# Multiples of the identity built on chip, first loads on two queues, three added groups of small matmuls and a new written-out order, in a fused attention and state-space kernel

## The chip, the cores and the metric

The kernel runs on one core of a Trainium2 chip. A core has five engines, each with an instruction stream of its own that it works through in order: PE (TensorE, matmuls), DVE (VectorE, elementwise work), ACT (ScalarE, activation functions and copies), POOL (GpSimd; here memsets and the issue of software DMAs) and SP (SyncE, issue of DMAs). They share an on-chip memory, SBUF, of 128 partitions and a small accumulator memory, PSUM, of eight banks. Streams wait for one another by semaphores. The metric is the device time of one execution in microseconds (us), as the median of several runs; smaller is better.

## The reference, cut to what matters

Two independent branches, whose outputs stand side by side in the last dimension:

```python
def _A_ref(x, wqkv, w_phi, wo):                 # linear attention, 16 heads of 28
    qkv = (x @ wqkv).reshape(B, S, 3, H, Dh)    # S = 2048, D = 448
    pq = einsum("bhsd,hdf->bhsf", q, w_phi)     # the same for k
    phi = concat([softmax(p), softmax(-p)])
    kv = einsum("bhsf,bhsd->bhfd", phi_k, v);  z = phi_k.sum(s)
    o = (phi_q @ kv) / (phi_q @ z + 1e-6)
    return o @ wo
def _B_ref(u, A, Bc, Cc, log_dt, Dskip):        # state-space convolution, 256 states
    K[d, l] = Re sum_n Cc * exp(dt * A * l) * dt * Bc      # l = 0..2047
    y = irfft(rfft(u padded) * rfft(K padded))[:L]         # along the sequence
    return y + u * Dskip
return concat([a, b], axis=-1)
```

All inputs and the output are bf16.

## The kernel before, in words

The convolution is done as a real discrete Fourier transform of 512 points on tiles of 128 partitions. Its parts are named by a label given with `step(...)`:

- **states**: six raw arrays (`rawAre`, `rawAim`, `rawCre`, `rawCim`, `rawBre`, `rawBim`, 448 x 256 each, 224 KB) are transposed and scaled by matmuls against a diagonal matrix `DT` (function `to_states`, label `st...`). `stAre` is what the step sizes act on, `stCre` and `stCim` are copied out of PSUM, `stB0` and `stB1` each read both `rawBim` and `rawBre`. Four products of them on DVE (`cb`) give the starting values. `hlA`, `lowA` (and `hlT`, `lowT`) store the decay in two bf16 parts.
- **phases** (`exps`, `rot`): for eight chunks of 56 channels the decay and the phase of a state are multiplied by 1 to 16. This is a matmul against `PID`, 16 multiples of the identity matrix, held as a 128 x 16 x 128 bf16 tile of 512 KB. Before the change `PID` is loaded from a constant in DRAM (unit 18, line 470), and `ident`, its first slice, by a transfer of its own (line 450).
- **hi, damp, far, build**: tables of powers (complex products on DVE, some of whose adds are accumulating DMAs that POOL issues, `add_to`, line 387), from which `build` makes the convolution kernel on PE.
- **sc / last, ks, conv, inv**: scatter to row positions by small DMAs, the kernel's spectrum, the product with the signal's spectrum (`us`, from `ua`, `ub` and the table `G1`, stored to DRAM and loaded again, `su`), and the inverse transform. The channels go through these in three groups (`GROUPS`, of four, two and two chunks).

The attention branch transposes x in 16 blocks (`xT`, from four loads `xs`, label `inx`), folds `w_phi` into the projections (`fold1` for keys, `fold0` for queries: transposes of `Wqk`, copies, then products with `BD`, a block matrix that four small DMAs, label `bd`, fill from `w_phi`), and then runs keys (`ke`, `kz`, `key`), `keyend` and queries (`qe`, `qz`, `q`). An exponential on ACT stands behind each `ke` and `qe`.

Nothing of the order of work follows from loops. The body builds a list of 1359 units, each with the engines that it may run on; `ORDER` (line 97) is a written-out string of unit numbers with a letter for the engine (P, D, A, G for POOL, S for SP), and `Plan.run` (line 213) emits the units in that order. Addresses in SBUF come from `HOMES`, PSUM banks from `BANKS`; both were written out by the same planner. Tiles share addresses where their lives don't overlap, so a transfer can have to wait until an older tile at its address has been read. The second number in each `plan.add` is the planner's cost, which the chip never sees. In the profile, line 360 is any ordinary matmul, 330 any `tensor_tensor`, 340 any activation, 346 and 351 copies, 384 any plain DMA, 398 and 396 the two forms of `add_to` (by POOL's accumulating DMA, by DVE), 608 the `xT` transposes, 618 the `fold` transposes, 649 the two gathers `ub`.

At the start of the kernel before, SP issues all first loads, in this order: `ldt`, `ident`, `Cim`, `bd`, `Are`, `Bim`, `Cre`, `Bre`, `bd`, x0, `Wqk` (784 KB), `bd`, `PID`, x1, `bd`, `HM`, ua1, ua0, `Aim`, `G1` (1 MB), `Wv`. POOL issues two gathers of 896 KB each in the meantime. `G1` shares an address with `f1`, a tile of the `cb` products. PE's order at the start is: `dt`, `stCim`, `stAre`, `stCre`, `stB0`, `lowA`, `stB1`, four `xT`, the `fold1` and `fold0` transposes, `exps0.1`, the `fold1` products, and so on to the first `ke0`.

Of the kernel before, what the change touches and what calls it, by code (L numbers as in the profile page):

```python
# [11 lines left out]
ACT = mybir.ActivationFunctionType  # L12
# [24 lines left out]
N_TB = 21  # L37
TB_STEP = 2368
# [15 lines left out]
def _dft_tables():  # L54
# [29 lines left out]
    pid = np.eye(128)[:, None, :] * np.arange(1, 17)[None, :, None]  # L84
# [13 lines left out]
0S 15G 24P 1S 5S 16G 19S 2S 7S 23D 25A 26D 54P 55A 4S 27P 29A 6S 52P 33D 53A 32A 30A 56P 34P 165G 57P 58D 20S 61D 8S  # L98
96P 31A 98P 12S 35A 92P 59D 94P 130P 97A 131D 95D 60D 21S 128P 142P 18S 99A 140P 124P 93A 141A 129D 143D 683P 126P
127D 144P 145D 146P 125A 684A 9S 22S 132P 685A 147D 133D 686A 138P 106P 134P 136P 107D 680P 135A 150P 137D 139D 102P  # L100
100P 63D 687A 62D 263P 681A 104P 105D 101D 151D 210G 211G 156S 682A 103D 209S 265A 213D 264A 257P 164S 254P 259A 258A
255A 260P 256A 309P 166G 262A 168D 300P 261A 152P 212D 167D 154P 311A 306P 303P 310A 153D 155D 285G 301A 279P 3S 13S
302A 148P 149D 307A 308A 28P 304A 287P 295P 280D 288D 305A 312P 39A 40A 266P 296D 313D 37A 36A 219P 267D 49A 41D 184P
185A 221P 186P 220A 191P 187A 38D 189P 190D 192A 14S 64D 65D 67G 284P 292P 46A 69D 251P 68D 43A 42A 271P 47A 222A 71G
48D 66D 223S 249P 50P 252A 294A 286A 272A 196P 246P 51A 174P 250A 179P 194P 80A 193S 195A 180A 247A 44D 176P 177A 244P
169P 201P 70D 197A 72D 82A 269G 73D 181P 268P 289D 188S 83D 182A 76D 75G 84D 77D 175D 45A 229P 171P 79D 202A 74D 183S
270A 78D 230A 276P 253S 199P 273D 81A 699D 245A 224P 248S 315G 200A 170A 86A 688P 277G 700D 278A 206P 203S 178S 225A
746D 226P 745D 172A 198S 274P 275P 239P 204P 281D 283P 747D 85A 87A 240A 89D 173S 205A 701G 227A 282P 690A 689A 691P
236P 744S 694A 693A 698S 207A 88D 291P 695A 293G 692A 749D 330P 322P 332A 290P 703D 234P 323G 237A 324A 702D 208S 748D
# [12 lines left out]
381D 862P 1020D 1052P 1021D 1012A 861A 1007A 863D 884S 1061D 1009A 1057A 1058A 415G 1031D 1049P 1078D 1055A 363P 364D
1053A 120P 121D 1032D 367P 1056A 1030D 1051A 1033D 398P 893S 422P 1022G 1054A 892G 890S 1023D 1050A 392P 1024D 900G
406P 1029G 400A 1059S 1062G 1064D 395P 399A 397A 366P 396A 1075G 424A 373D 401P 403A 1063D 402A 371P 430P 1035D 379P
393A 394A 1077D 432A 387P 404P 425P 1025G 372A 426D 380A 405D 1026D 409P 1065G 899G 375P 383P 423G 374P 408A 886S 382P
410A 433P 417P 1178P 1034D 878S 419D 388A 447P 434A 407G 411D 391P 1036G 427D 1180A 390P 1027D 418A 1227P 1067D 435D
1066D 1028G 1179A 412P 1076D 873G 413P 420P 421P 429P 1228A 1231A 1230A 444P 448A 875G 428P 1068G 453P 437P 1229A
1079D 450P 449A 895G 1197D 894S 436P 931S 455A 902G 1181P 454A 445A 452A 1198D 879G 1081D 881S 1080D 1069D 1070D 441D
1071D 1182A 451A 446A 442D 1073D 1037P 1072D 880S 1196G 937S 1184A 1224P 1039P 1185A 882G 1225A 1183A 885S 1226A 439D
1074D 1199G 1082G 1038A 1040A 1189P 1200D 1235P 1201D 950S 1191A 1186P 1188A 1083P 1187A 1195A 17G 1202D 870G 887G  # L130
868G 869S 484P 440D 1203D 1204D 438D 1194A 1205G 1239A 1212G 1190A 866S 1192A 1085P 1215D 485A 1084A 1232P 1193A 864G
1086A 1113S 1088G 1237A 1213D 1233A 874S 1214D 1117S 901G 1238A 943S 1234A 896G 867S 1216D 1207D 1206D 621P 502P 1240A
624P 1217D 508P 1109G 1208D 1218D 1087S 1241A 877S 1210D 1114G 925S 618P 1236A 504A 1209D 563P 503A 1219D 883S 898G
1098S 627P 628A 629A 505P 1211D 619A 1244D 506A 919S 1242G 1243D 626A 1245G 1110S 511P 949S 1222P 163S 623A 904S 625A
1258G 443D 510A 888S 1220P 1259D 162S 509A 513A 1260D 1124G 622A 507A 464P 1261D 920S 897S 512A 876G 620A 560P 903S
1262D 926S 1247D 482P 472P 938S 1221A 1223A 914S 514P 494P 630P 483D 465A 565A 908S 871G 891G 865G 1091S 666P 889S
561A 1246D 564A 515D 158S 516D 495D 631D 473A 667A 872D 1094G 474P 475A 632D 517D 532P 533A 566P 569P 550P 562A 568A
570A 567A 1248G 542P 571A 913S 1264D 456P 457D 1263D 492P 1099S 493A 927P 656P 551A 458D 462P 543A 1097G 928D 907S
1104G 939P 1250D 633D 157S 1120S 646P 522P 1249D 1251D 1252D 1253D 940A 657A 518D 572P 932S 1126S 463A 1090G 944S 160S
600P 636P 637A 578P 579A 1127G 1265G 1112S 601A 1121S 519D 1111S 647A 915P 1093G 929P 530P 930A 523A 951P 921P 1089S  # L140
459D 916A 1119G 580P 581A 540P 933P 1101G 658P 1100S 952A 668P 1254D 1115G 1256D 1255D 541A 659D 520P 945P 922A 531A
460D 1102G 934A 1257D 909P 669A 638P 648P 521A 649A 906G 573D 552P 1266P 574D 534D 1092S 910A 1268P 610P 1107A 634D
1122S 635D 650D 461D 905S 941P 1103S 670D 553A 1108A 1118A 159S 676S 496D 575D 639D 576D 544D 946A 1267A 1269A 1296G
476D 554D 1300A 953P 1095D 486D 524D 911P 935P 611A 912A 660D 1271G 608P 923P 924D 609A 577D 917P 671P 161S 954A 555P
1096S 466D 582D 918A 672A 651P 1293G 1305S 487P 612D 677S 640D 942A 556A 661P 467P 947P 557P 1308S 497P 678S 1116G
936A 1106G 955D 1105S 662A 956D 477P 948A 1276G 468A 1288G 588P 488A 598P 590P 652A 589A 525P 478A 1270G 958G 489P
498A 673P 1303G 490A 1294A 613P 674A 479P 599A 591D 1287S 675A 535P 583P 957D 536A 1275G 1125G 641P 469P 480A 537P
1291G 653P 642A 1286G 526A 558A 1272S 584A 585P 1307S 499P 614A 973D 1299A 1279G 527P 975D 959D 615P 1123S 1283A 654A
960D 491A 1289S 1134P 962D 1138P 1304A 481A 586A 592D 1281S 1273G 528A 961D 1290S 963P 964A 470D 593P 545P 1298G 977G
1285G 974D 976D 538A 1135A 1292S 1295A 1130P 594A 1274S 643P 1128S 500D 1139A 965P 1131D 1306S 1142P 1302A 546A 547P  # L150
1277G 978D 980D 1278D 616A 1280S 966A 1143A 1136P 970P 1282G 679S 595P 979D 1129S 602D 982D 1132P 644A 1137A 1309S
1284G 1144P 1146D 981D 1297A 971A 471A 1140P 1145A 1334D 984D 1311P 1315P 596A 1319P 1141A 1147D 1323P 1316D 1171D
1310S 1148D 1133A 1162D 1163D 990P 1352D 501A 1301S 603P 1317P 1161D 1312A 1320A 983G 1321P 1313P 1150D 968P 1314A
1324A 597S 1149G 991A 1325P 1160D 1327D 1328D 1330D 1332D 1329D 1165G 548D 1164G 987P 529S 1151D 1152G 1322A 1326A
# [45 lines left out]
class Plan:  # L200
# [5 lines left out]
    def step(self, label):  # L206
        self.label = label
# [70 lines left out]
def kernel(  # L278
# [172 lines left out]
    for nm in RAW:  # L451
        step("in" + nm)
        dma(["SP"], raw[nm][0:112, :, :], srcs[nm].rearrange("(j p) n -> p j n", p=112), w=[raw[nm][0:112, :, :]])
# [646 lines left out]
```

## Time and profile before

| | |
|---|---|
| median of 3 runs | 293.46 us (292.38 to 295.47) |
| profiled execution: its own time | 294.26 us |
| profiled execution: span, first to last instruction | 292.5 us |
| mean granted TensorE clock in it | 0.969 of full speed |
| busy: PE / DVE / ACT / POOL | 258.8 / 258.1 / 230.0 / 84.1 us |
| moved by DMA | 44.15 MB |

The span lies inside the execution's own time; 1.8 us are around it. Busy time counts an engine while an instruction of it runs, whether it is held up inside or not. In the rows of a timeline the first number is the start in us from the start of the span, the second the time from the start of the first to the end of the last of the instructions that the row puts together, then engine, line, operation, output and input with shapes, and their number; in square brackets the idle time ahead of it and what ended that. In a table by stretches, each engine has its busy time and the number of its instructions, then come the granted TensorE clock, the mean busy share of the 16 DMA engines and GB/s.

### The profile page before, as it was taken

How to read it: one execution, taken by the hardware profiler on the slowest of the kernel's cores; microseconds unless marked ns; L12 is line 12 of the kernel's file. 1: busy time of each engine (PE TensorE's matmuls, PEld its weight loads, DVE VectorE, ACT ScalarE, POOL GpSimd, SP SyncE). 2: the span in 40 equal slices, each digit the busy share in tenths (PEclk: the TensorE clock that was granted, in tenths of full speed). 3: DMA queues.
4: the chain of work that ended last, by engine and by line, in shares of the span. 5: the costliest groups of instructions: out<-in, count | busy, mean ns of one | idle time of the engine just before them, and what ended most of it. 6: DMA issues, size and time to landing. Idle time of an engine off the chain costs nothing.

```text
span 292.5 us, 10350 instructions
## 1 busy us (share of the span) xinstructions
PE 258.8 (88%) x4440; PEld 214.0 (73%) x4440; DVE 258.1 (88%) x346; ACT 230.0 (79%) x385; POOL 84.1 (29%) x135
## 2 busy tenths in 40 slices
PE   3758999987865989799999999999996999989994
PEld 2747665544554987588858898688995968879993
DVE  0545999899989999999999999999995999989990
ACT  3844999999899997999999999999862965533222
POOL 1300004101235212212224862564503284022300
PEclk9975999999997999999999999999997999999999
DMA  5993603894997737423166862567755868996953
GB/s 156 241 388 98 201 3 49 116 228 142 199 270 132 125 73 176 79 37 65 24 118 123 131 127 58 120 134 175 157 176 217 294 111 153 345 240 132 197 133 96
DMA packets 41781, 44.15 MB, mean 151 GB/s; under 512 B 18849, under 2 KB 37542, under 8 KB 41350
## 3 DMA queue, kind: packets, MB, share of 16 engines
q0 software_dynamic: 12320, 17.47, 33.9%
q1 hardware_dynamic: 24038, 24.02, 27.3%
q10 hardware_dynamic: 5376, 1.99, 2.7%
q8 instruction: 35, 0.57, 0.8%
q14 instruction: 12, 0.10, 0.1%
HBM read 19.71 MB, written 7.34 MB: 92 GB/s over the span
## 4 chain that ended last, share of the span: by engine, by line
PE 48%; ACT 14%; DVE 14%; DMA 14%; issue 8%; SPq 1%; POOL 0%; DVEq 0%; ACTq 0%; POOLq 0%
PE psum L360 46%; DVE sbuf L330 11%; ACT sbuf L340 8%; DMA sbuf<-sbuf 6%; DMA sbuf<-in_A_w_phi_dram 5%; ACT sbuf L351 4%; SPq L384 1%; DMA sbuf<-in_B_B_im_dram 1%; DMA SUd<-sbuf 1%; ACT sbuf L346 1%; DVE sbuf L396 1%; ACT L340 1%; PE psum L608 1%; DVE sbuf L806 1%; PE psum L819 1%
## 5 line engine op out<-in xcount | busy, mean ns | idle before, releaser
L360 PE MATMUL psum<-sbuf 128*32 128x49 bf16 (+11 forms) x4216 | 247.0, 258 | 24.9 <-ACT sbuf L340 4.7
L360 PEld LDWEIGHTS <-sbuf 128*128 128x128 bf16 (+5 forms) x4216 | 200.9, 121 | 66.8 <-issue 22.6
L330 DVE TENSOR_TENSOR sbuf<-sbuf 128x896 bf16<-128x896 bf16 (+8 forms) x233 | 195.9, 900 | 6.6 <-DMA sbuf<-sbuf 3.3
L340 ACT ACTIVATE sbuf<-psum 128x896 bf16<-128x896 f32 (+4 forms) x189 | 123.2, 803 | 5.7 <-PE psum L360 4.6
L351 ACT CAST sbuf<-psum 128x448 bf16<-128x448 f32 (+3 forms) x155 | 78.7, 611 | 46.2 <-PE psum L360 34.5
L398 POOL DMA_DIRECT2D sbuf<-sbuf x43 | 43.4, 1036 | 163.5 <-DVE sbuf L330 108.0
L384 POOL DMA_DIRECT2D sbuf<-sbuf x56 | 35.8, 818 | 9.9 <-ACT sbuf L351 9.3
L351 DVE CAST sbuf<-psum 128x448 bf16<-128x448 f32 (+2 forms) x29 | 17.5, 614 | 9.3 <-PE psum L360 6.2
L396 DVE TENSOR_TENSOR sbuf<-sbuf 128x896 bf16<-128x896 bf16 (+2 forms) x27 | 22.0, 823 | 0.2
L351 ACT COPY sbuf<-psum 128x896 bf16<-128x896 bf16 (+2 forms) x18 | 14.3, 858 | 2.7 <-PE psum L618 2.6
L351 DVE COPY sbuf<-psum 112x512 bf16<-112x512 bf16 (+2 forms) x22 | 9.4, 454 | 5.4 <-PE psum L618 4.0
L340 ACT ACT_TABLE_LOAD x9 | 11.5, 1283 | 0.9 <-PEq L1084 0.7
L819 PE MATMUL psum<-sbuf 112*128 112x112 bf16 x128 | 8.4, 212 | 1.0 <-ACT sbuf L351 0.7
L819 PEld LDWEIGHTS <-sbuf 112*128 112x128 bf16 x128 | 7.3, 97 | 2.7 <-issue 1.4
L330 DVE TENSOR_TENSOR sbuf<-psum,sbuf 128x896 f32<-128x896 f32 (+3 forms) x12 | 7.0, 591 | 1.7 <-PE psum L360 1.5
L608 PE MATMUL psum<-sbuf 128*112 128x128 bf16 x64 | 6.4, 242 | 1.4 <-ACT sbuf L351 1.4
L608 PEld LDWEIGHTS <-sbuf 128*112 128x112 bf16 x64 | 5.6, 151 | 2.0 <-issue 1.5
L346 ACT CAST sbuf<-sbuf 128x1792 bf16<-128x1792 f32 x3 | 5.6, 1869 | 0.0
L816 POOL MEMSET sbuf<- 128x16 bf16 x16 | 4.5, 385 | 2.1 <-DVE sbuf L334 1.8
L618 PE MATMUL psum<-sbuf 112*112 112x112 bf16 x32 | 2.7, 248 | 2.3 <-DMA sbuf<-in_A_wqkv_dram 2.2
L346 DVE CAST sbuf<-psum 128x896 bf16<-128x896 f32 x1 | 1.1, 1092 | 4.1 <-ACT sbuf L340 4.1
L736 POOL MEMSET sbuf<- 128x224 bf16 x8 | 4.7, 590 | 0.0
(22 smaller groups left out, 35.5 us busy)
## 6 DMA issues: line engine op xcount, KB each, us to landing
sbuf<-sbuf POOLq DMA_DIRECT2D x15, 448.0 KB, 4.9
sbuf<-sbuf POOLq DMA_DIRECT2D x29, 224.0 KB, 3.9
SUd<-sbuf SPq DMA_DIRECT2D x16, 224.0 KB
sbuf<-const SPq DMA_DIRECT2D x3, 1024.0 KB
sbuf<-const SPq DMA_DIRECT2D x17, 160.0 KB
sbuf<-SUd SPq DMA_DIRECT2D x3, 896.0 KB
sbuf<-in_A_x_dram SPq DMA_DIRECT2D x4, 448.0 KB
sbuf<-in_B_u_dram SPq DMA_DIRECT2D x2, 896.0 KB
```

Source lines behind the costliest of these rows:

```text
L330: lambda e: nc.vector.tensor_tensor(out=at(out_), in0=at(a), in1=at(b), op=op), [whose(a), whose(b)], [out_])
L340: lambda e: nc.scalar.activation(at(out_), at(a), func, scale=scale, bias=bias), [whose(a)], [out_],
L346: lambda e: (nc.scalar.copy if e == "ACT" else nc.vector.tensor_copy)(at(out_), at(a)), [whose(a)], [out_])
L351: lambda e: (nc.scalar.copy if e == "ACT" else nc.vector.tensor_copy)(at(out_), at(a)), [whose(a)], [out_])
L360: nc.tensor.matmul(out_, lhsT=lhsT, rhs=rhs, start=start, stop=stop, **kw)
L384: plan.add({**also, **{e: own[e] for e in engs}}, fn or (lambda e: QUEUES[e].dma_start(out=out_, in_=in_, **kw)), r, w, mode=k, load=wire, ...
L396: nc.vector.tensor_tensor(out=out_, in0=out_, in1=in_, op=ALU.add)
L398: nc.gpsimd.dma_start(out=o, in_=i, max_dma_last_dim=3584, accum_op=ALU.add)
L608: mms(p, [lambda t, j=j, x=x: nc.tensor.transpose(t[:, j, :], x[:, 112 * j:112 * j + 112], ident[:, :]) for j in range(4)], 0.22, [x, iden ...
L736: pool(0.2, lambda en: nc.gpsimd.memset(w[:, :, ZERO, :], float(np.sqrt(0.5))), [], [w[:, :, ZERO, :]])
L816: pool(0.2, lambda e, V=V: nc.gpsimd.memset(V[:, D_HEAD, :], 1.0), [], [V[:, D_HEAD, :]])
L819: mms(pk, [lambda t, s=s, c=c, ts=ts: nc.tensor.transpose(t[:, s, 112 * c:112 * c + 112], EKT[:, s, c, ts], id112) for s in range(2) for c ...
```

## The change

1. `PID` and `ident`: the constant in DRAM shrinks to the identity (32 KB). Its load fills `ident`; `PID` is made by a copy and four adds that double the number of slices.
2. The loads at the start may be issued by SP or ACT, and the new order gives five of them to ACT: `ident`, `Are`, `Cim`, `Bim`, `Bre`.
3. Twenty-four units `fill` are new, each of eight 128x128 matmuls of the identity with itself, whose result nobody reads. A unit that the order gives to POOL emits nothing. The order gives three to PE: 181 and 174 ahead of `stAre`, and 179 among the `us` units of the signal's spectrum.
4. `ORDER`, `HOMES` and `BANKS` are new as a whole, by the same planner with transfers taken to land later.

The diff (unit numbers from 19 on are 4 higher than before, from the signal's spectrum on 28 higher):

```diff
+N_FILL = 24
...
-    pid = np.eye(128)[:, None, :] * np.arange(1, 17)[None, :, None]
+    pid = np.eye(128)
...
 ORDER = """
-0S 15G 24P 1S 5S 16G 19S 2S 7S 23D 25A 26D 54P 55A 4S 27P 29A 6S 52P 33D 53A 32A 30A 56P 34P 165G 57P 58D 20S 61D 8S
-96P 31A 98P 12S 35A 92P 59D 94P 130P 97A 131D 95D 60D 21S 128P 142P 18S 99A 140P 124P 93A 141A 129D 143D 683P 126P
...
+0S 1A 18D 19D 20D 21D 16G 191G 2A 23S 5A 7A 4S 27D 24S 6A 15G 28P 12S 181P 25S 184G 29A 174P 30D 31P 56P 57D 8S 34A
+37D 35A 33A 58P 59A 61P 38P 36A 39A 22D 60P 134P 17G 135A 144P 145A 63D 130P 64D 711P 131A 132P 128P 9S 65D 100P 62D
+177G 146P 715A 133D 714A 96P 102P 150P 129D 147D 97D 98P 26S 103D 713A 99D 140P 142P 136P 712A 151D 160S 137A 143D
+141A 101D 138P 192S 66D 708P 108P 104P 109D 193G 106P 105D 67D 238G 110P 139A 282P 107D 709A 148P 194G 3S 175G 710A
+291P 149D 284A 285P 111D 288P 195D 237S 154P 283A 334P 331P 239G 196D 240D 293A 292A 286A 287A 289A 337P 290A 13S 155D
...
-    dma(["SP"], ident[:, :], P_d[:, 0, :], w=[ident[:, :]])
+    dma(["SP", "ACT"], ident[:, :], P_d, w=[ident[:, :]])
...
-        dma(["SP"], raw[nm][0:112, :, :], srcs[nm].rearrange("(j p) n -> p j n", p=112), w=[raw[nm][0:112, :, :]])
+        dma(["SP", "ACT"], raw[nm][0:112, :, :], srcs[nm].rearrange("(j p) n -> p j n", p=112), w=[raw[nm][0:112, :, :]])
...
     step("pid")
-    dma(["SP"], PID[:, :, :], P_d, w=[PID[:, :, :]])
+    acopy(PID[:, 0, :], ident[:, :])
+    for n in (1, 2, 4, 8):
+        tt(PID[:, n:2 * n, :], PID[:, 0:n, :], PID[:, n - 1, :].unsqueeze(1).to_broadcast([128, n, 128]), ALU.add)
...
+    for i in range(N_FILL):
+        step(f"fill{i}")
+        p = ps([128, 128])
+
+        def busy(e, p=p):
+            if e == "PE":
+                for _ in range(8):
+                    mm(p.t, ident[:, :], ident[:, :], True, True)
+        plan.add({"PE": 0.48, "POOL": 0.0}, busy, [ident[:, :]], [p])
```

In the new order SP issues `ldt`, `bd`, `Cre`, `bd`, `Wqk`, `bd`, x0, x1, `bd`, `HM`, ua0, `Aim`, ua1, `G1`, `Wv`. PE starts with `dt`, two fills, `stAre`, `stCre`, `stCim`, `stB1`, `lowA`, `stB0`, then three `fold` transposes, `exps0.1`, two transposes, `xT2`, a transpose, `xT0`, `xT3`, a transpose, `xT1`, the four `fold1` products, `exps0.0`, four `xT`, and the first `ke0`. DVE starts with four `PID` units, `negid`, `DT`, the copy of `stCre`, `hlA`, the last `PID` unit, four `cb`, and then copies of `fold` and `xT` and two more `cb` up to `ab`, which combines `ua` and `ub`. `G1` shares its address with no tile of the start any more; ua1 does with `rawBim` and the copy of `stCim`, and `Wv` with the copy of `stCre`.

149 lines of the change are left out of this document (74 added, 75 removed), and 57 rows, old and new, of the table HOMES.

## The prediction

> **What bounds the kernel now.** I read the page's head first, then a table by stretches, then the chain of work that ended last, then the timeline of the start.
>
> ```profile
> span 292.5 us, 10350 instructions
> ...
> PE 258.8 (88%) x4440; PEld 214.0 (73%) x4440; DVE 258.1 (88%) x346; ACT 230.0 (79%) x385; POOL 84.1 (29%) x135
> ```
>
> PE and DVE are level at 88%, so the question is where their missing 34 us lie. The table by stretches (busy time of PE, PEld, DVE, ACT, POOL, then clock, DMA share, GB/s) tells it:
>
> ```profile
> 0.00:30.00 30.00, 19.29 (x201) 17.07 (x202) 13.35 (x23) 16.14 (x23) 3.32 (x11) 0.83 0.76 219
> 30.00:60.00 30.00, 29.62 (x259) 17.94 (x258) 28.72 (x32) 29.97 (x50) 4.93 (x4) 1.00 0.47 99
> 60.00:176.00 116.00, 101.17 (x2044) 82.83 (x2042) 113.23 (x149) 112.32 (x173) 37.19 (x62) 0.99 0.63 126
> 176.00:215.00 39.00, 38.94 (x828) 33.73 (x829) 38.67 (x57) 36.94 (x73) 17.89 (x29) 1.00 0.54 121
> 215.00:257.00 42.00, 39.00 (x610) 32.74 (x609) 37.95 (x51) 24.58 (x51) 15.41 (x24) 0.96 0.80 234
> ```
>
> In the first 30 us DVE lacks 16.7 us, ACT 13.9 and PE 10.7. From 30 to 215 DVE lacks 1.3, 2.8 and 0.3 us: it is full, and so nearly is ACT. From 176 on PE is full. So this is a slow start ahead of a full kernel, and a us saved at the start moves everything behind it, if the full part takes as long as before. The chain agrees (start, length, what):
>
> ```profile
> 8.37 14.35 DMA sbuf<-in_A_w_phi_dram
> ...
> 176.06 44.25 PE psum L360 x969
> ```
>
> It passes the start through one transfer, the last small `bd` piece, issued at 8.37 and waited for until 22.7. The timeline shows the work around it:
>
> ```profile
> 4.43 0.93 PE L360 MATMUL psum<-sbuf 112*128 112x112 bf16 x8 [1.85 <-DMA sbuf<-in_B_C_im_dram]
> ...
> 7.72 4.71 PE L360 MATMUL psum<-sbuf 112*128 112x112 bf16 x56 [1.00 <-DMA sbuf<-in_B_C_re_dram]
> 12.49 1.05 PE L608 MATMUL psum<-sbuf 128*112 128x128 bf16 x16
> 15.74 1.53 PE L618 MATMUL psum<-sbuf 112*112 112x112 bf16 x20 [2.19 <-DMA sbuf<-in_A_wqkv_dram]
> 17.98 1.48 PE L360 MATMUL psum<-sbuf 128*128 128x112 bf16 x16 [0.70 <-DMA sbuf<-const]
> ...
> 27.51 1.51 PE L360 MATMUL psum<-sbuf 112*112 112x512 bf16 x4
> ```
> ```profile
> 30.81 4.09 DVE L330 TENSOR_TENSOR sbuf<-sbuf 128x1792 bf16<-128x1792 bf16 x4
> ```
> ```profile
> 29.05 8.03 ACT L340 ACTIVATE sbuf<-psum 112x512 bf16<-112x512 f32 x16 [0.80 <-PE psum L360]
> ```
>
> PE waits in turn for `Cim`, `Cre`, `Wqk` (until 15.74), `PID` (17.98) and `bd` (22.86). My two marks are the first `ke0` on PE, 27.51, behind which ACT is full, and the end of `ab` on DVE, 30.81 + 4.09 = 34.90.
>
> **The change, part by part.** *PID on chip.* Its 512 KB leave the queue ahead of x1 and the last `bd`. The sums of bytes come from the shapes in the code. Before, up to and with `PID` the queue held 32 + 5 x 224 + 448 + 784 + 512 = 2896 KB, landed at 17.98. After, everything ahead of the last `bd` on both queues is 32 + 5 x 224 + 784 + 2 x 448 = 2832 KB, so it comes near 17.9 instead of 22.7 from this alone. What it costs DVE:
>
> ```profile
> L351 DVE COPY sbuf<-psum 112x512 bf16<-112x512 bf16 x11 | 4.5, 417 | 1.2 <-PE psum L608 1.2
> L330 DVE TENSOR_TENSOR sbuf<-sbuf 128x448 bf16<-128x448 bf16 x8 | 3.0, 387 | 0.2
> L330 DVE TENSOR_TENSOR sbuf<-sbuf 128x896 bf16<-128x896 bf16 x112 | 64.6, 618 | 4.4 <-PE psum L360 2.2 <-DMA sbuf<-sbuf 2.0
> ```
> ```profile
> 2.86 0.20 DVE L476 TENSOR_SCALAR sbuf<-sbuf 128x128 bf16<-128x128 bf16 x1 [2.86 <-DMA sbuf<-const]
> ...
> 7.71 1.09 DVE L346 CAST sbuf<-psum 128x896 bf16<-128x896 f32 x1 [4.12 <-ACT sbuf L340]
> ```
>
> Copy and adds of 128 to 1024 elements: 0.2 + 0.2 + 0.28 + 0.42 + 0.7 = 1.8 us between these rows' sizes. DVE sits idle for 4.12 us there, so I cost them at nothing. Four stand ahead of `negid` and `DT`; `ident` lands near 2.4 (2.86 before, issued 0.4 later), so they end at 3.6, and `DT` waits for ACT longer than that. Without the cover they cost 1.8.
>
> *Two queues.* The DMA engines' share in the first us (stretches as above):
>
> ```profile
> 2.00:3.00 1.00, 0.53 (x4) 0.44 (x4) 0.14 (x2) 0.20 (x2) 0.00 (x0) 1.00 0.34 93
> 3.00:4.00 1.00, 0.00 (x0) 0.00 (x0) 0.59 (x2) 0.00 (x0) 0.00 (x0) 1.00 0.76 201
> 4.00:5.00 1.00, 0.57 (x7) 0.58 (x8) 0.00 (x0) 0.00 (x0) 0.00 (x0) 1.00 0.88 261
> ```
>
> From 4 on the engines are near full. Twice the rate of issue can fill only what is missing here: 0.66 + 0.24 + 0.12, about 1.0 us. So the last `bd` comes at 17, give or take 1.
>
> But ACT pays for its issues. It now emits five DMAs ahead of its first activation:
>
> ```profile
> 0.74 1.28 ACT L340 ACT_TABLE_LOAD   x1 [0.74 <-PEq L1084]
> ```
> ```profile
> 4.03 0.49 SPq L384 DMA_DIRECT2D sbuf<-in_B_B_re_dram  x1
> ```
>
> Five times up to 0.49 is 2.4 us, with the table load 3.7, so `dt`'s exponential ends near 4.6 and `DT` (0.62) at 5.2, against 3.59 before. Queued behind: `stAre`, and everything on PE. It begins at 5.2, where before `stCim` began at 4.43 but PE waited again until 7.72 for `Cre`, which is now SP's third. `stAre`, `stCre`, `stCim` end at 7.5. Nothing is lost.
>
> Next on PE stands `stB1`, which needs `Bim` and `Bre`, now the last two of ACT's queue. Here the change decides. ACT's queue holds 928 KB in rows of 512 bytes; SP's, beside it, `Wqk` in rows of 1792 and x in rows of 3584. With equal shares `Bre` lands when 2 x 928 KB have moved, at 0.26 MB/us from 2.6: 9.7. Two stretches show how two queues share (queue, packets, MB, share of the engines):
>
> ```profile
> q0 software_dynamic: 116, 0.82, 66.0%
> q1 hardware_dynamic: 143, 0.39, 36.1%
> ```
> ```profile
> q1 hardware_dynamic: 1220, 0.90, 54.0%
> q0 software_dynamic: 172, 1.01, 49.4%
> ```
>
> The first (15 to 18 us, q1 with rows of 4096 and 3584 bytes) is close to one packet each, 116 and 143. The second (18 to 23, q1 with rows of 896) has seven small for each large one, and time about halved. The second is the nearer to small rows beside large ones, so I take near-equal shares and 1 us for the slower small rows: 10.7. The ends are 9.7 and 15.3 (below).
>
> From there PE's stream runs without a wait that I can see, `bd` at 17 included. `stB1`, `lowA`, `stB0` are 48 matmuls at 4.71/56 = 84 ns, 4.0; 28 `fold` transposes at 1.53/20 = 77 ns, 2.1; 32 `xT` transposes at 66 ns, 2.1; two `exps` at 1.48, 3.0; 16 `fold1` products at 84 ns, 1.3. Sum 12.5: the first `ke0` at 23.2, 4.3 earlier. PE has done the same by then, to within half a us. DVE: a `cb` takes
>
> ```profile
> 10.35 3.21 DVE L330 TENSOR_TENSOR sbuf<-psum,sbuf 128x896 f32<-128x896 f32 x3 [1.54 <-PE psum L360]
> ```
>
> 1.07. Four of them end at 10.7 + 4.0 + 2 x 1.07 = 16.8; up to `ab` follow five `fold` copies at 0.39, seven `xT` at 0.42, a product's copy at 0.62 and two `cb`, 7.7; `ab` with one copy 4.7. End 29.2, against 34.90: 5.7 earlier, with about as much done, as three more `xT` stand against three fewer `fold` copies.
>
> *Clock and fills.* The clock fell to half at the start:
>
> ```profile
> 18.40:28.80 10.40, 8.12 (x76) 7.44 (x74) 5.48 (x10) 5.24 (x7) 0.00 (x0) 0.52 0.58 199
> ```
>
> It fell after PE had been mostly idle from 13.5 on. In the new order PE would sit idle from 7.5 to 10.7, and the fall may come then. The two fills run near 3 to 5, at 116 ns each 1.9 us, hidden by `stAre`'s wait for `DT`; they come too early for that gap. Transposes in it took 1.33/12 = 111 ns, against 77 ahead of it:
>
> ```profile
> 19.25 1.33 PE L618 MATMUL psum<-sbuf 112*112 112x112 bf16 x12
> ```
>
> So 6 us at half speed cost 1.9. I take half of that, 1.0, as this trace can't say if the clock falls. The third fill, 0.9 us at most, lies among `us`, where PE lacks 15 of 116 us: nothing.
>
> *G1 free of f1.* It was issued only at 28.3, when the last `cb` had been read:
>
> ```profile
> 28.29 0.34 SPq L384 DMA_DIRECT2D sbuf<-const  x1
> ```
>
> Now it waits behind ua1, for the `cb` at 16 or so. It lands earlier by more than `us` moves. Nothing.
>
> *The rest of the order.* Counted from the two strings: 25 copies go from ACT to DVE and 29 back, one accumulate more goes to DVE. At some 0.6 us each that is 2 us off DVE, which the `PID` units put back at the start. In both orders `build4`, `conv1` and `conv2` stand after the same share of each engine's units, to within two or three us of work. I take nothing; the bounds are 3 us either way, about what DVE lacks from 60 to 176.
>
> **Sum.** PE's mark: 4.3 - 1.0 = 3.3. DVE's: 5.7, less the same 1.0 for evictions that come later, 4.7. Mean 4.0, against the profiled execution's 294.26 (span 292.5 and 1.8 around it): 290.3. That execution lies 0.8 above the median, so on the median 293.46 - 4.0 = 289.5 us.
>
> **The rivals.** *Bre is starved (slower).* If the queues take turns row by row, as 116 against 143 suggests, `Are` and `Cre` (480 KB) end at 4.4, `Wqk` with `Cim` at 8.3, and while both x move (896 KB, to 12.2) `Bim` gets an eighth, 128 KB. The other 320 KB then go beside gathers, which held 66% of the engines: a third of 0.26 is 0.09 MB/us, and some of the 320 have moved before the gathers are in full flow, so 15.3. PE then stands from 7.5 to 15.3, surely at half clock for 10 us, as before (3.2). First `ke0`: 15.3 + 12.5 + 3.2 = 31.0, 3.5 later than before: 297.0. It decides from `Bre` at 27.5 - 12.5 - 3.2 = 11.8 on. The Trainium skill, page "DMA: Bandwidth & Descriptors", section "Queues, rings and completion order", speaks for it: an SDMA engine goes round-robin between its queues packet by packet, so a queue of short rows gets the fewer bytes. By that rule alone the time would be this rival's; the trace agrees from 15 to 18 and not from 18 to 23, where the packets stood 1220 to 172. Chance 0.2.
>
> *The loads share evenly and the clock holds.* `Bre` at 9.7, no fall: PE 5.3, DVE 6.7 earlier, and up to 1.5 from a fuller middle: 286 us. For it: the second stretch above, where time is halved between the queues. Chance 0.2.
>
> *The middle takes it back.* DVE is at 98% from 60 to 176, and every wait on an accumulating DMA counts there. Two of
>
> ```profile
> 81.39 7.07 DMA sbuf<-sbuf
> ```
>
> with a cover of some 5 us leave 4 us: 293.5, no change. Against it stand DVE's waits for such DMAs in the whole kernel before (total, times, longest):
>
> ```profile
> DVE sbuf L330 <- DMA sbuf<-sbuf: 3.3, 4, 1.6
> ```
>
> Chance 0.2. My forecast, 289.5 with a range of its own of 287.5 to 292, has 0.4.
>
> **How the numbers follow.** A measurement of this kernel can tell about 1% from no change, 2.9 us: faster is below 290.5, slower above 296.4. The forecast's 0.4 is 0.28 faster and 0.12 same; the even start 0.19 and 0.01; the middle 0.05, 0.13 and 0.02; the starved queue 0.02, 0.04 and 0.14. Faster 0.54, same 0.30, slower 0.16. The range goes from 283, the even start with the middle's 3 us, to 297.
>
> **What would show it.** In the changed profile: PE's first `ke0` at 23 to 25 and `ab` ended near 30; no matmul waiting for a constant; the last `bd` near 17; PE's longest early wait on `Bre`, ended near 11. If that wait ends after 12, the starved queue is right. If `ke0` starts at 24 and the span is still 292, the middle took it. The prediction is wrong as a whole if the full part, from `ab`'s end to the end, doesn't take the 257.6 us of before to within 3.

## The result, and the profile after

| | before | after |
|---|---|---|
| median of 20 executions each | 293.42 us | 292.19 us |
| lowest to highest | 291.61 to 297.66 | 287.50 to 297.06 |
| ratio after / before, 95% interval | | 0.987 (0.983 to 0.991) |
| profiled execution: own time, span | 294.26, 292.5 us | 287.50, 285.7 us |
| the same kernel again on another chip (run e8 below): median, ratio | 294.12 us | 291.56 us, 0.997 (0.992 to 1.001) |

By the ratio the change makes the kernel 1.3% faster in the first measurement; in the second it is 0.3%, which can't be told from nothing. The ratio takes only the executions within 1.5% of each kernel's fastest (in the first measurement 17 of 20 before, 8 of 20 after), while the medians are over all. The medians differ by 1.2 and 2.6 us (0.4 and 0.9%). 289.5 us was forecast: the first ratio, 0.987 of 293.42, would be 289.6 us, and the median of all is 292.19. The changed kernel's executions lie further apart than those of before, and the profiled one is the fastest of its 20: its 6.8 us must not be read as the gain. So a second profile of the same kernel stands beside it below. Its execution took 290.34 us, the second fastest of its 12, so no profile shows what an execution near the median does.

The page's head of the changed kernel:

```profile
span 285.7 us, 10405 instructions
...
PE 255.0 (89%) x4464; PEld 210.4 (74%) x4464; DVE 260.0 (91%) x348; ACT 228.9 (80%) x389; POOL 84.7 (30%) x136
```

(Lines have moved by two to four: 362 is any matmul here, 332 any `tensor_tensor`, 348 and 353 copies, 386 any plain DMA, 398 and 400 `add_to` by DVE and POOL, 612 and 622 the transposes of x and `Wqk`; in the experiments they lie a few lower.) The work is nearly the same: PE has 3.8 us less of it, DVE 1.9 us more. The table by stretches, in the columns explained above:

```profile
0.00:30.00 30.00, 22.09 (x239) 18.20 (x240) 19.44 (x34) 19.21 (x32) 3.77 (x12) 1.00 0.87 246
30.00:60.00 30.00, 26.29 (x250) 16.12 (x248) 28.20 (x31) 27.97 (x44) 5.18 (x7) 1.00 0.45 70
60.00:176.00 116.00, 103.14 (x2208) 85.30 (x2209) 113.73 (x149) 114.94 (x181) 36.51 (x61) 1.00 0.56 117
176.00:215.00 39.00, 37.37 (x780) 31.90 (x775) 36.45 (x57) 34.98 (x71) 18.10 (x27) 1.00 0.68 168
215.00:257.00 42.00, 41.77 (x612) 35.57 (x602) 40.32 (x49) 24.55 (x51) 16.17 (x24) 1.00 0.81 217
```

The first 30 us hold 6.1 us more of DVE's work and 3.1 more of ACT's than before, and the clock there is 1.00, not 0.83. From 30 to 60 both engines hold less than before (DVE 28.20 against 28.72, ACT 27.97 against 29.97), and from 176 to 215 DVE 2.2 us less. The chain that ended last now reaches back only some 20 us, to an accumulating DMA (first and last long piece):

```profile
263.64 5.78 DMA sbuf<-sbuf
...
277.67 4.68 PE psum L362 x80
```

It says nothing of the start any more. The start shows in PE's timeline:

```profile
5.50 1.84 PE L362 MATMUL psum<-sbuf 112*128 112x112 bf16 x16 [0.98 <-DVE sbuf L332]
...
10.21 0.27 PE L362 MATMUL psum<-sbuf 112*128 112x112 bf16 x1 [1.73 <-DMA sbuf<-in_B_B_im_dram]
13.20 3.97 PE L362 MATMUL psum<-sbuf 112*128 112x112 bf16 x47 [2.72 <-DMA sbuf<-in_B_B_re_dram]
...
17.67 0.95 PE L362 MATMUL psum<-sbuf 128*128 128x112 bf16 x16
18.46 0.77 PE L622 MATMUL psum<-sbuf 112*112 112x112 bf16 x8
...
20.46 2.22 PE L362 MATMUL psum<-sbuf 112*112 112x112 bf16 x32
22.52 1.06 PE L612 MATMUL psum<-sbuf 128*112 128x128 bf16 x16
23.41 1.03 PE L362 MATMUL psum<-sbuf 112*112 112x512 bf16 x4
...
41.57 4.53 PE L362 MATMUL psum<-sbuf 128*128 128x112 bf16 x31 [2.65 <-DVE sbuf L332]
```

`Bim` is waited for until 10.21 and `Bre` until 13.20; behind them PE waits for nothing that the rows show until 38, for the last `bd` (20.46) neither; the first `ke0` is at 23.41, 4.1 us earlier than before. Near 40 stands a wait that before doesn't have: PE idle for 2.65 us, until 41.57, for DVE. DVE's mark, the end of `ab`, is 29.42 + 1.08 = 30.50, 4.4 us earlier. In DVE's timeline, with the five `PID` instructions (the copy at 2.61, three adds, the last at 9.38) and `DT` (4.82):

```profile
2.61 0.20 DVE L348 COPY sbuf<-sbuf 128x128 bf16<-128x128 bf16 x1 [2.61 <-DMA sbuf<-const]
2.84 1.01 DVE L332 TENSOR_TENSOR sbuf<-sbuf 128x128 bf16<-128x128 bf16 x3
...
4.82 0.63 DVE L332 TENSOR_TENSOR sbuf<-sbuf 112x448 bf16<-112x448 bf16 x1 [0.86 <-ACT sbuf L342]
...
9.38 0.68 DVE L332 TENSOR_TENSOR sbuf<-sbuf 128x1024 bf16<-128x1024 bf16 x1
...
29.42 1.08 DVE L332 TENSOR_TENSOR sbuf<-sbuf 128x1792 bf16<-128x1792 bf16 x1
```

**The second profile of the same kernel** has a span of 288.6 us. Its `ab` ends at 30.89, but its stretch from 215 to 257 is another one:

```profile
215.00:257.00 42.00, 39.95 (x583) 34.04 (x576) 38.91 (x48) 22.18 (x46) 16.20 (x24) 0.96 0.75 204
...
245.50:249.00 3.50, 3.50 (x27) 2.80 (x26) 3.47 (x4) 1.98 (x4) 0.58 (x1) 0.51 0.95 367
```
```profile
29.81 1.08 DVE L332 TENSOR_TENSOR sbuf<-sbuf 128x1792 bf16<-128x1792 bf16 x1
...
240.67 3.10 DVE L332 TENSOR_TENSOR sbuf<-sbuf 128x896 bf16<-128x896 bf16 x3 [2.04 <-DMA sbuf<-sbuf]
```
```profile
245.08 12.12 PE L362 MATMUL psum<-sbuf 112*128 112x448 bf16 x130 [2.05 <-DVE sbuf L353]
```

In order: DVE waits 2.04 us for an accumulating DMA, PE then waits 2.05 us for DVE, and right after that the clock is at half for 3.5 us. In the fastest execution nothing of this stands there: PE is busy for 41.77 of these 42 us.

### The profile page after: what moved, and what is told of

It is laid out like the page before. It is cut to its first block, busy times and chain, and to the rows that moved or that the text cites. A ratio compares the mean times of both kernels' runs of the same rounds, so it can differ in the third digit from the quotient of the medians.

```text
span 285.7 us, 10405 instructions
## 1 busy us (share of the span) xinstructions
PE 255.0 (89%) x4464; PEld 210.4 (74%) x4464; DVE 260.0 (91%) x348; ACT 228.9 (80%) x389; POOL 84.7 (30%) x136
## 5 line engine op out<-in xcount | busy, mean ns | idle before, releaser
L362 PEld LDWEIGHTS <-sbuf 128*32 128x32 bf16 (+5 forms) x4240 | 198.7, 120 | 68.5 <-issue 23.3
L332 DVE TENSOR_TENSOR sbuf<-sbuf 128x896 bf16<-128x896 bf16 (+10 forms) x237 | 197.9, 890 | 9.6 <-ACT sbuf L342 4.2
L353 ACT CAST sbuf<-psum 128x448 bf16<-128x448 f32 (+3 forms) x164 | 82.2, 587 | 40.2 <-PE psum L362 37.4
L398 DVE TENSOR_TENSOR sbuf<-sbuf 128x896 bf16<-128x896 bf16 (+2 forms) x28 | 23.6, 851 | 0.2
L353 DVE CAST sbuf<-psum 128x448 bf16<-128x448 f32 (+2 forms) x20 | 12.2, 628 | 1.3 <-issue 1.1
L353 ACT COPY sbuf<-psum 128x896 bf16<-128x896 bf16 (+2 forms) x15 | 11.5, 831 | 0.7 <-PE psum L362 0.5
L820 POOL MEMSET sbuf<- 128x16 bf16 x16 | 6.0, 487 | 17.7 <-DVE sbuf L332 17.1
L348 ACT CAST sbuf<-psum 128x896 bf16<-128x896 f32 x2 | 1.8, 907 | 4.9 <-PE psum L362 4.9
L336 DVE SCALAR_TENSOR_TENSOR sbuf<-sbuf 128x64 f32<-128x64 f32 (+2 forms) x7 | 4.1, 590 | 0.0
```

The lines of the kernel that those rows point to most:

```text
L332: lambda e: nc.vector.tensor_tensor(out=at(out_), in0=at(a), in1=at(b), op=op), [whose(a), whose(b)], [out_])
L348: lambda e: (nc.scalar.copy if e == "ACT" else nc.vector.tensor_copy)(at(out_), at(a)), [whose(a)], [out_])
L353: lambda e: (nc.scalar.copy if e == "ACT" else nc.vector.tensor_copy)(at(out_), at(a)), [whose(a)], [out_])
L362: nc.tensor.matmul(out_, lhsT=lhsT, rhs=rhs, start=start, stop=stop, **kw)
L398: nc.vector.tensor_tensor(out=out_, in0=out_, in1=in_, op=ALU.add)
L820: pool(0.2, lambda e, V=V: nc.gpsimd.memset(V[:, D_HEAD, :], 1.0), [], [V[:, D_HEAD, :]])
```

## The experiments

Twelve runs follow, of nine new kernels: e8 is the changed kernel again, e10 repeats e7 and e11 repeats e5. They ran on four chips: e1, e3, e4 and e5 on one, e2, e6, e7 and e8 on another, e9, e10 and e11 on a third, e12 on a fourth. Each ratio is to the kernel before on the same chip; a comparison across chips goes by these ratios and is the weaker for it.

**e1: the multiples on chip, alone.** The kernel before, in its old order; `PID` is no load any more but five DVE instructions behind `DT`.

```diff
-    dma(["SP"], PID[:, :, :], P_d, w=[PID[:, :, :]])
+    copy of ident, then four adds on DVE, as in the change
 ORDER:
-... 18S ...
-... 26D ...
+... 26D 18D ...
```

> The kernel before with one part of the change alone: the 16 multiples of the identity are made on DVE right behind DT, and their 512 KB leave the load queue; order, addresses and the single queue are those of before. Theory (the start goes through): the last bd lands near 18 instead of 22.7, the first ke0 is at 24 to 25 instead of 27.5, and the span is 2 to 3.5 us shorter than before. Rival (the new order of the middle made the gain, the start alone does nothing): ke0 earlier, but the time within 1 us of before.

Measured: 288.52 us against 293.37, ratio 0.981 (0.974 to 0.987). This small part gives at least as much as the whole change (0.987 and 0.997, on other chips; the first interval touches this one). PE's timeline in it:

```profile
18.11 0.59 PE L356 MATMUL psum<-sbuf 112*112 112x112 bf16 x8
...
20.68 1.02 PE L356 MATMUL psum<-sbuf 112*112 112x512 bf16 x4
```
```profile
0.00:30.00 30.00, 22.89 (x266) 18.84 (x267) 21.26 (x37) 22.72 (x37) 3.33 (x11) 1.00 0.83 246
```

The products with `bd` run at 18.11 without a wait (before: 22.86, after one), the first `ke0` at 20.68 instead of 27.51, and the clock of the first 30 us is 1.00, not 0.83. The forecast of this run had 24 to 25 for the `ke0` and 2 to 3.5 us for the time; the median falls by 4.9. The mark moves by more than the time, 6.8 us, and part of that is the clock, which ran at half for 10.4 us at the start of the kernel before. (The profiled execution, 290.15 us, is the longest of its six.) So taking the 512 KB off the queue is enough for the gain, and the rest of the change adds none to it.

**e2: two queues, alone.** The kernel before, with `ident`, `Are`, `Cim`, `Bim`, `Bre` issued by ACT as in the change.

```diff
 ORDER:
-0S ... 1S 5S ... 2S 7S ... 6S ...
+0S 1A 2A 5A 7A 6A ...
```

> The kernel before with the second queue alone: ident, Are, Cim, Bim and Bre are issued first of all by ACT, everything else (PID of 512 KB from DRAM, the order, the addresses) is that of before. Theory (short rows on ACT's queue starve beside x0, Wqk and PID on SP's): Bre lands at 12 or later instead of 8 or earlier, PE waits for it, the first ke0 is at 27 to 30 and the time 0 to 3 us longer than before. Rival (two queues gain the issue time): Bre by 9, the first ke0 at 26.5 or earlier, the time 1 us shorter.

Measured: 294.34 us against 294.12, ratio 0.998 (0.993 to 1.003): nothing. Neither expectation came in full: `Bre` lies between the two, the first `ke0`, at 26.24, goes with the rival, and the time isn't 1 us shorter. Its PE:

```profile
11.66 4.66 PE L356 MATMUL psum<-sbuf 112*128 112x112 bf16 x48 [3.08 <-DMA sbuf<-in_B_B_re_dram]
...
22.50 0.59 PE L356 MATMUL psum<-sbuf 112*112 112x112 bf16 x8 [1.94 <-DMA sbuf<-in_A_w_phi_dram]
```

`Bre` comes at 11.66, but the last `bd` still at 22.50, as with one queue (22.7): the same bytes stand ahead of it, and issuing them on two queues brought it at most 0.4 us. The forecast's "about 1.0 us" for the faster rate of issue isn't there.

**e3: `Bre` alone back on SP,** behind `Cre` and ahead of `Wqk`; all else as in the change.

```diff
 ORDER:
-... 24S 6A 15G ...
+... 4S 6S 27D 24S 15G ...
```

> The kernel after with one load moved: rawBre is issued by SP right behind rawCre and ahead of Wqk, and no more as the last of ACT's queue. Theory (the two long waits of PE, until 10.2 for Bim and until 13.2 for Bre, come from short rows sharing with longer ones, and each us there is paid by the whole kernel): Bim and Bre land by 8 to 9, the first ke0 is at 19 to 21 instead of 23.4, the span 2.5 to 4 us shorter than after. Rival (DVE and ACT or the other loads set ke0 anyway): ke0 at 22.5 or later and the time within 1 us of after.

**e5: all first loads on SP,** in the order `ldt`, `ident`, `Are`, `bd`, `Cre`, `Cim`, `Bim`, `Bre`, `bd`, `Wqk`, ...; all else as in the change.

```diff
 ORDER:
-0S 1A 18D ... 2A 23S 5A 7A 4S 27D 24S 6A ...
+0S 1S 2S 18D ... 23S 4S 5S 7S 6S 27D 24S ...
```

> The kernel after with all first loads back on SP: ident and Are behind ldt, and Cim, Bim, Bre behind Cre and ahead of Wqk; nothing else changes. Theory (the second queue gains at most 1 us of issue time and costs more by starving Bre): Bre lands near 8 to 9, PE doesn't wait until 13.2, the first ke0 is at 20 to 22, the span 1 to 3 us shorter than after. Rival (the second queue is the source of the gain): all loads land later by 1 us or more, ke0 at 24 or later, the time 1 us or more longer than after.

Measured, beside one another: e3 288.06 us, ratio 0.979 (0.973 to 0.985); e5 287.38, ratio 0.979 (0.973 to 0.984); before 293.37. PE in e3 (the first `ke0`) and in e5:

```profile
20.73 1.03 PE L358 MATMUL psum<-sbuf 112*112 112x512 bf16 x4
```
```profile
9.80 4.57 PE L358 MATMUL psum<-sbuf 112*128 112x112 bf16 x47 [0.66 <-DMA sbuf<-in_B_B_re_dram]
...
19.28 1.79 PE L358 MATMUL psum<-sbuf 112*112 112x112 bf16 x32 [1.28 <-DMA sbuf<-in_A_w_phi_dram]
...
21.80 1.03 PE L358 MATMUL psum<-sbuf 112*112 112x512 bf16 x4
```

On one queue `Bre` comes at 9.80 instead of 13.20, though it stands behind all the same small loads, and the first `ke0` at 21.80 instead of 23.41. In e3, which keeps the other four loads on ACT's queue, `ke0` comes at 20.73, behind a wait for `Bim` until 9.95, and the ratio is the same. (8 to 9 was expected for `Bim` and `Bre` in both.) So the second queue by itself shows no cost; what costs is `Bre` at its end, beside SP's `Wqk` and x, which PE needs later. How the two queues shared the engines is in the changed kernel's trace, from 8 to 12 us (ACT's queue is q10, SP's q1; packets, MB, share of the engines):

```profile
q1 hardware_dynamic: 468, 0.73, 83.4%
q10 hardware_dynamic: 455, 0.22, 28.0%
```

They move one packet for one, and SP's, with the longer rows, take three times the bytes and the time. The Trainium skill, page "DMA: Bandwidth & Descriptors", section "Queues, rings and completion order", says that a DMA engine takes turns between its queues packet by packet; 468 against 455 agree with it, and the near-equal shares of time that I had taken don't.

Both profiles have the wait near 40 still, and here the clock falls behind it; e5 from 30 to 60:

```profile
30.00:60.00 30.00, 26.29 (x224) 15.30 (x222) 25.42 (x28) 25.15 (x37) 5.18 (x7) 0.89 0.43 61
```

DVE has 2.8 us less work done there than in the changed kernel's fastest execution (28.20), ACT the same 2.8 less: the 1.6 us by which its first `ke0` comes earlier are given back here. (This execution, 288.87 us, is the longest of its six.)

**e4: no fills.** The three groups go to POOL, where they emit nothing.

```diff
 ORDER:
-... 181P ... 174P ... 179P ...
+... 181G ... 174G ... 179G ...
```

> The kernel after without the three groups of small matmuls (24 matmuls left out; nothing else changes). Theory (they lie where PE waits and too early for the gap of 8.5 to 13.2): granted clock, first ke0 and time as in the kernel after, to within 1 us. Rival (they keep the clock up): the clock falls to half somewhere in the first 25 us, the first ke0 comes 1 to 2 us later and the time is 1 to 3 us longer than after.

Measured: 290.10 us, ratio 0.984 (0.977 to 0.991), no worse than the changed kernel with fills (0.987 and 0.997, on other chips). In its profile `Bre` came only at 15.70, and PE stood nearly idle for 7.5 us; still the clock of the first 30 us is 1.00:

```profile
10.53 0.28 PE L358 MATMUL psum<-sbuf 112*128 112x112 bf16 x1 [2.64 <-DMA sbuf<-in_B_B_im_dram]
15.70 4.57 PE L358 MATMUL psum<-sbuf 112*128 112x112 bf16 x47 [4.89 <-DMA sbuf<-in_B_B_re_dram]
```
```profile
0.00:30.00 30.00, 17.19 (x203) 15.34 (x204) 16.34 (x30) 16.00 (x25) 3.65 (x11) 1.00 0.82 246
```

Three profiles with the fills have `Bre` at 13.05 to 13.52. In this one the last 25 packets of ACT's queue fall between 12 and 16 us, where the gathers of POOL hold 42% of the engines' time and then 86%; in the changed kernel's first profile the gathers hold 10% from 12 to 14. What brought the one or the other isn't settled. The first `ke0` follows `Bre` and is at 26.63, 3.2 us later than in the changed kernel, which neither expectation had; this execution, 292.10 us, is the longest of its six.

**e6: the wait near 40.** PE waits there with `lowT` (unit 54), which the change's order puts behind DVE's products for `H1` (72 and 73). One unit is moved; the first loads stay on two queues.

```diff
 ORDER:
+... 54P 72D ...
-... 54P ...
```

> The kernel after with one unit moved: the matmuls lowT stand ahead of the two DVE products H1 in the order, so that they no longer wait for the second product; addresses, engines and all else as after. Theory (PE's idle 2.7 us near 39 come from that wait, and in most executions the clock falls to half there, which is a large part of the spread of 287.5 to 297): no gap of PE over 1.5 us between 34 and 46, the clock at 1.00 from 30 to 60, the median 1.5 to 4 us under that of after on the same chip. Rival (DVE and ACT set the pace there, or the spread comes from the landing of Bre alone): the median within 1 us of after.

**e7: both,** e5's loads and e6's unit.

> Both: all first loads on SP with Bim and Bre ahead of Wqk, and lowT ahead of H1. Theory: the two losses add, as one is the landing of Bre and the other the stretch from 36 to 46; first ke0 at 21 to 22, clock at 1.00 throughout the first 60 us, the median near 284 to 285.5, 2 to 3.5 under the kernel with one queue alone (287.4) and the fastest so far. Rival: within 1 us of 287.4.

**e8: the changed kernel again,** nothing edited.

> The kernel after once more, as the measure for the others of this chip and a second look at how Bre lands. Theory (its landing on ACT's queue varies from execution to execution, 13.2 in the first profile and 15.7 in that without the small matmuls): Bre lands somewhere from 12.5 to 16.5, and the first ke0 follows it by 10 to 11 us; the median 290 to 292.5. Rival: landing and ke0 as in the first profile to within 0.5 us.

Measured, beside one another: e6 288.58 us (286.85 to 289.98), ratio 0.989 (0.983 to 0.995); e7 286.25 (284.26 to 286.65), ratio 0.979 (0.972 to 0.986); e8 291.56 (289.57 to 294.84), ratio 0.997 (0.992 to 1.001); before 294.12. PE and the stretch in e6:

```profile
38.86 5.56 PE L358 MATMUL psum<-sbuf 112*128 112x112 bf16 x40 [0.95 <-ACT sbuf L349]
```
```profile
30.00:60.00 30.00, 27.40 (x259) 16.86 (x258) 29.39 (x32) 29.23 (x46) 5.18 (x7) 1.00 0.46 70
```

The wait near 40 is gone in e6, DVE and ACT hold 1.2 us more from 30 to 60, and the median is 3.0 us below e8's. So 1.2 us of it is seen; the other 1.8 isn't in this stretch. (Of the two profiles, e8's also has the waits of 2.04 and 2.05 us near 240, and e6's hasn't.) The forecast held: no gap of PE over 1.5 us, a clock of 1.00. That the clock falls there in most executions of the changed kernel isn't shown: in both of its profiles it is 1.00.

e6 and e7 differ by the first loads alone: no execution of e7 (284.26 to 286.65) is as long as the shortest of e6 (286.85), so the queues and the order of the first loads cost 2.3 us on the medians. e7's first `ke0` is at 20.91 and its clock 1.00 as expected, but its median lies over the 284 to 285.5 of the forecast, 1.1 us below e5's on another chip: that the two gains add in full isn't shown.

That `lowT` waited because `H1` writes into the tile that it reads is how I read the code; the run shows that their order makes the wait.

e8's `Bre` lands at 13.52, against 13.20, and its first `ke0` comes at 23.80, against 23.41: within the half us of its rival, so these two profiles don't show that the landing varies much.

**e9, e10, e11: e7 without fills, e7 again, e5 again,** beside one another.

> The kernel with all first loads on SP and the `lowT` unit moved ahead, without the three PE fills: it leaves out 24 matmuls whose result nobody reads. Theory (the fills are worth nothing): within 1 us of the same kernel with them, run beside it, clock 1.00 in the first 30 us. Rival (the fills keep the clock up): the clock falls below 0.95 in the first 30 us and the median is 1.5 us or more above the one with fills.

> All first loads on SP and the `lowT` unit moved ahead, again, beside the kernel without fills and the one with `lowT` unmoved. Theory (both waits were real costs): median 285.5 to 287, spread under 3 us, 1 us or more below the kernel with all first loads on SP alone. Rival (`lowT` costs nothing once the loads are early): within 0.5 us of it.

> All first loads on SP alone, `lowT` where the change has it. Theory (the wait of `lowT` brings the clock down): the profile shows PE idle for 2.5 us or more before 42 and a clock of 0.89 to 0.94 from 30 to 60; median 287 to 288.5. Rival: the clock is 1.00 there, and the median within 0.5 us of the kernel with `lowT` moved.

Measured: e9 285.36 us (283.64 to 290.17), ratio 0.971 (0.963 to 0.979); e10 288.78 (285.31 to 290.17), ratio 0.980 (0.970 to 0.991); e11 287.66 (286.57 to 289.06), ratio 0.983 (0.977 to 0.990); before 292.50. No gain from the fills shows: without them the median is lower, by more than the 1 us that was expected, and the clock of the first 30 us is 1.00 in each of the three. The expectations of e10 failed: the same kernel that gave 286.25 gives 288.78 here, over its upper end, above e11.

Over both runs of each (10 executions) e7's kernel has a median of 286.4 and e5's of 287.4; that `lowT` costs something once the loads come early isn't shown. e11's profile is as its theory had it: PE idle for 2.66 us until 39.26, and a clock of 0.94 from 30 to 60. e7's profile has a wait of DVE of 1.59 us for an accumulating DMA near 235 and a clock of 1.00 behind it; e10's has the waits of the second profile above, and 0.96 from 215 to 257:

```profile
238.66 3.10 DVE L328 TENSOR_TENSOR sbuf<-sbuf 128x896 bf16<-128x896 bf16 x3 [2.04 <-DMA sbuf<-sbuf]
```
```profile
243.07 17.13 PE L358 MATMUL psum<-sbuf 112*128 112x448 bf16 x202 [2.05 <-DVE sbuf L349]
```

**What that wait hangs on.** The late DMA is a 448 KB accumulation issued by POOL near 229. Beside it SP loads the second of two 1024 KB tables (`GI`). Issues of both and the landing, in the fastest execution of the changed kernel and in the second profile of the same kernel:

```profile
220.67 7.12 SPq L386 DMA_DIRECT2D sbuf<-sbuf  x9
227.90 0.39 SPq L386 DMA_DIRECT2D sbuf<-const  x1
...
229.73 0.98 POOL L400 DMA_DIRECT2D sbuf<-sbuf  x1 [2.73 <-ACT sbuf L353]
...
sbuf<-sbuf POOLq DMA_DIRECT2D x1, 448.0 KB, 5.8
```
```profile
221.42 8.84 SPq L386 DMA_DIRECT2D sbuf<-sbuf  x9
230.38 0.39 SPq L386 DMA_DIRECT2D sbuf<-const  x1
...
230.48 0.98 POOL L400 DMA_DIRECT2D sbuf<-sbuf  x1 [1.61 <-ACT sbuf L353]
...
sbuf<-sbuf POOLq DMA_DIRECT2D x1, 448.0 KB, 10.2
```

The same, read from each profile of the order of the change:

| | after | e9 | e6 | e3 | e4 | e5 | e11 | e8 | e7 | e10 |
|---|---|---|---|---|---|---|---|---|---|---|
| table issued ahead of the accumulation by, us | 1.83 | 1.53 | 1.42 | 1.28 | 1.12 | 0.60 | 0.48 | 0.10 | 0.01 | -0.15 |
| accumulation lands after, us | 5.8 | 6.4 | 6.4 | 6.6 | 6.8 | 9.3 | 8.6 | 10.2 | 9.7 | 10.2 |
| DVE then waits, us | 0 | 0 | 0 | 0 | 0 | 1.18 | 0.48 | 2.04 | 1.59 | 2.04 |

With a lead of 0.60 us or less the accumulation takes 2 to 4 us longer than with one of 1.12 or more, and DVE waits. Within one kernel the lead went from 1.83 to 0.10, as SP's nine small transfers ahead of the table took 7.12 us in the one execution and 8.84 in the other; what slowed them isn't shown. That leaves a rival: the nine took 7.12 to 7.82 us in the five profiles in which the accumulation landed early and 8.35 to 9.08 in the five others, so what slowed them may have slowed the accumulation too.

**e12: the table earlier.** e9's kernel, `GI` (unit 704) issued three small transfers earlier.

```diff
 ORDER:
+... 704S 1323S ... 1154S ... 1316S ...
-... 1323S ... 1154S ... 1316S ... 704S ...
```

> All first loads on SP, `lowT` moved ahead, no PE fills (24 matmuls whose result nobody reads are left out), and the second 1024 KB table `GI`, which SP loads near 227, issued three small transfers earlier. In ten profiles the 448 KB accumulating DMA that POOL issues near 229 landed after 5.8 to 6.8 us where `GI` had been issued 1.1 us or more ahead of it, and after 8.6 to 10.2 us where it was 0.6 us or less ahead. Theory (the two transfers get into each other's way): SP issues `GI` near 224.5, the accumulating DMA lands within 7 us, DVE has no wait for a DMA of 1 us or more from 230 to 245, and the executions lie closer together, within 4 us, at a median of 284 to 286. Rival (`GI` can't go earlier, as the tile at its address is still read): SP issues it near 226.8 as before and holds up the small transfers behind it; median 285.5 to 288.

Measured: 284.71 us (283.19 to 287.52), ratio 0.972 (0.966 to 0.979); before 293.30. The issues and the landing:

```profile
223.49 0.37 SPq L382 DMA_DIRECT2D sbuf<-const  x1
...
227.91 0.98 POOL L396 DMA_DIRECT2D sbuf<-sbuf  x1 [2.29 <-ACT sbuf L349]
...
sbuf<-sbuf POOLq DMA_DIRECT2D x1, 448.0 KB, 4.7
```

With a lead of 4.42 us the accumulation lands after 4.7 us, the fastest of these eleven profiles, and no wait of DVE for a DMA stands between 225 and 249. The address was free. The small transfers were quick in this profile too (six in 4.52 us ahead of the table), so it doesn't exclude the rival above. The spread is 4.3 us, a little over the 4 that were expected; the median is 0.65 below e9's, from another chip, so the gain in time itself isn't established by this pair. It has the lowest median of all that ran, 8.6 us below before.

## Why the prediction came out as it did

The sign was right. The time was in the wide range, 283 to 297; by the first ratio, 289.6 us, it meets the forecast of 289.5, but the median of all executions, 292.19, lies just over the forecast's own 287.5 to 292, and the second measurement shows less. The way there was right in parts.

- **`PID` on chip**: right, and by e1 enough for the whole gain. The five instructions ran from 2.61 to 3.85 and at 9.38, 1.9 us in all against 1.8, under DVE's waits for ACT and PE. `bd` was no longer waited for. That it came near 17 isn't shown, only that it was there by 20.46.
- **`DT` at 5.2, nothing lost**: it ended at 5.45, and PE's stream began at 5.50. Right.
- **The faster rate of issue, 1.0 us**: wrong, by e2 at most 0.4 us.
- **`Bre` at 10.7**: wrong, 13.20. The failed step is "so I take near-equal shares and 1 us for the slower small rows". The two stretches of the profile that I weighed spoke for different sides, and I chose the wrong one: the changed kernel's queues moved 468 and 455 packets from 8 to 12 us, one for one. The range of landing that I gave, 9.7 to 15.3, held it.
- **12.5 us from `Bre` to `ke0`**: wrong, 10.21 (13.20 to 23.41). I had priced two `exps` at 1.48 us each, from a row (17.98) that ran into the half clock of before, 18.40 on; in the new profile the one that stands by itself took 0.79 to the next start (17.67 to 18.46). The 16 `xT` transposes ahead of `ke0` took 0.89 to the next start, 56 ns each, not 66. And the **fall of the clock**, 1.0, didn't come. So `Bre` came 2.5 us later than forecast and the work behind it took 3.3 less. That the two cancelled was luck, and the two marks, 23.41 and 30.50, lie within 0.8 and 0.3 us of the forecast's 24.2 and 30.2 by it.
- **"Bre is starved"**: its transfers went its way, one packet for one and past its point of decision of 11.8, yet not its time. `Bre` came at 13.20 and not at 15.3: ACT's queue moved 0.22 MB from 8 to 12 us, where the rival had given it 128 KB while x moves, and only 12 packets were left for the time after. And the point of decision stood on the 12.5 and on 3.2 us of half clock, neither of which came; so "if that wait ends after 12, the starved queue is right" was a wrong sign.
- **The full part**: 288.6 - 30.89 = 257.7 us in the second profile, against 257.6 before. Between these two executions the change is worth the 3.9 us of span that its start brings, as the sum had it (4.0). The medians of that measurement differ by 2.6 us, as the one execution lies 0.8 us above the median of its first three runs and the other 1.2 below its own; what the longer executions lose isn't shown. The fastest execution has 255.2: it has neither the DVE wait at 238.6 nor the fall.
- **"The rest of the order: nothing, 3 either way"**: held as a bound in the two profiles, but two mechanisms were in it that I hadn't seen, the `lowT` wait and the accumulation beside the table. The latter is the rival "the middle takes it back" in kind, 2.04 us for a cover that was too short, though after 215 and not from 60 to 176.
- **G1 and fills at nothing**: no run speaks against it; e4 and e9 show nothing lost without the fills. For `G1` no run was made.

## What to carry to other kernels

Read the bytes ahead of the last transfer that the start waits for, and take them away: a constant that DVE can build in 1.9 us of idle time was worth 2% by itself here, and the rearrangement built around it added nothing. A second load queue was worth nothing where the DMA engines were near full (e2), and a load in short rows at its end came 3.4 us later than on one queue in the order of need (13.20 against 9.80). So put what is wanted first ahead of the large transfers. Where one kernel's executions differ by 2 or 3%, compare two profiles of that kernel with each other before explaining its difference from another one.

## What the runs showed of the hardware that was not expected

A gap in PE's work doesn't settle the clock. In the changed kernel 2.65 us of idle time near 40 left it at 1.00 in both profiles, and in e4 at the start 2.64 and 4.89 us with 0.28 us of work between them did; but 2.66 us and less were followed by half clock in e3, e4, e5 and e11, and 2.05 us in the second profile. The low stretch there lasted 3.5 us (0.51 from 245.5 to 249.0); that of e5, of 0.78, 0.50, 0.50 and 0.51 in the four stretches of 2 us from 38 to 46, was twice as long. The Trainium skill, page "TensorE: Matmul & The Clock Gate", section "What's actually happening", has a free-running window of about 3.4 us, and half clock after an idle one. The length of the stretches, one window and two, agrees, and that the same gap falls differently into such a window would fit the difference between executions, which isn't shown; that a gap must fill the window isn't what these runs show, since 2.05 us were enough.

The clock doesn't explain how far the executions of one kernel lie apart. Of the 20 of the changed kernel the two with a mean clock of 1.00 are the shortest, 287.50 and 287.51 us; but the nine with 0.993 or 0.994, about what one such stretch makes of the mean, lie anywhere from 288.50 to 294.21.

An accumulating transfer of 448 KB that was issued within 0.6 us of a load of 1024 KB landed after 8.6 to 10.2 us, and after 4.7 to 6.8 where the load had a lead of 1.12 us or more. That the one transfer slows the other is likely but not shown, as the small transfers ahead of the load were slower in the same profiles.
